# Per-head keys, values and w_in loaded as they are and converted on the engines

## The chip, the cores and the metric

The kernel runs on one core of a Trainium2 chip. Its work is spread over five engines that run at the same time and wait for each other through semaphores: TensorE (PE in the profile, its weight loads PEld), VectorE (DVE), ScalarE (ACT), GpSimd (POOL) and SyncE (SP). DMAs are issued from the instruction queues of SyncE, ScalarE or GpSimd, and their bytes are moved by 16 DMA engines that all issuers share. The metric is the device time of one execution in microseconds; less is better.

## What is computed

A retention layer (attention with a decay instead of a softmax) over 8 batches of 8 heads, 576 positions and 64 features, then a feed-forward layer with a hard-swish between two matrices, over all 4608 tokens:

```python
    batch, n_heads, seq, head_dim = (8, 8, 576, 64)
    n_tokens, d_model, d_ff = (4608, 512, 2048)
...
    scores = scale * np.matmul(q, k.transpose(0, 1, 3, 2))
    gamma = 1.0 - 2.0 ** (-5.0 - np.arange(H, dtype=np.float32))
    rel = pos[:, None] - pos[None, :]
    Dmat = np.where(rel >= 0, gamma[:, None, None] ** rel[None, :, :], 0.0)
    ret = scores * Dmat[None, :, :, :]
    return np.matmul(ret, v).astype(np.float32)
...
    h = x @ w_in
    relu6 = np.clip(h + 3.0, 0.0, 6.0)
    g = h * relu6 / 6.0
    return (g @ w_out).astype(np.float32)
```

All inputs and the output are float32; the matrix products on the chip run on float16 operands, so every operand is converted somewhere on its way.

## The kernel before

The 576 positions of a batch are 64 + 512. The first 64 positions of all eight batches together are one block of 512 tokens, block 0 (the "heads" of the sequences, in names hk, hq, hv). The other 512 positions of each batch are blocks 1 to 8, each cut into four chunks of 128 positions, loaded as fk, fq and fv by `load` (lines 166 to 180). For every block the kernel forms the retention output transposed (`xT`), multiplies it by w_in in 16 units ("up", products `ph`, 8 matmuls a unit), applies the hard-swish on ScalarE and VectorE (lines 514 and 516) and multiplies by w_out ("down", products `pd` and `pm`). From block 2 on the down product uses a Strassen scheme with sums of w_out (`ws`).

The order of work is written out by hand from line 749: `manual_schedule` keeps the instructions of each engine in the order of the text. So an instruction that waits holds up everything that stands behind it in its engine's queue, DMA issues included.

The part that the change touches is the beginning, up to the fifth unit of the up product of block 0:

- `indices` (line 89) and `distances` (line 107): small constants. The distances lie in `early`, a buffer of the tag "fv", which has four (IOB, line 56).
- Loads of the heads (lines 753 to 769): four pairs of batches, i = 0 to 3, each in two halves e. All queries and the first keys are loaded as float32 by SyncE and ScalarE. The keys of pairs 1 to 3 (`load_half`, line 394) and all values (`load_values`, line 439) are issued by GpSimd straight into float16 tiles, so that the DMA converts them. `behind` means that a DMA is issued only after another one has landed (`after`, line 389).
- `win_piece` (line 675) and `wout_piece` (line 683): w_in in four pieces of 512 columns and w_out in four pieces, all issued by GpSimd and converted by the DMA. Piece n of w_in serves the units 4n to 4n + 3 of the up product of block 0.
- `mask_of_heads` (line 115): ScalarE makes the decay masks of two heads a call from the distances; the four calls stand among other ScalarE work.
- `cast_heads` (line 414) converts a float32 head tile on VectorE: the first keys and all queries. `turn_heads` (line 419) transposes keys and queries on PE and copies them back on ScalarE. `picks` (line 435) fills `pick`, a selection matrix that GpSimd cleared before (line 767). `scores_heads` (line 464) forms scores and multiplies them by the masks on VectorE; `values_heads` (line 449) brings the values to chunk order with `pick`; `inner_heads` (line 477) makes `xT`.
- `decays`, `mask_of_chunk`, `decays_of_chunk` (lines 120 to 138): constants that the later chunks need, made on GpSimd behind the w_out issues (lines 817 to 819).
- `fetch(8, wout[0])` (line 820): SyncE loads chunks 4 to 7 once the first piece of w_out has landed.
- `idle_products` (line 379): products that nobody reads.

The order of PE at the beginning is: idle products, turns of keys and queries of pairs 0 to 3 with the scores of the pairs between, values, inner products, then the first four up units side by side, one quarter of the depth at a time, then one unit after another.

Of the kernel before, what the change touches and what calls it, by code (L numbers as in the profile page):

```python
# [12 lines left out]
FP32 = mybir.dt.float32  # L13
# [3 lines left out]
ALU = mybir.AluOpType  # L17
# [4 lines left out]
def kernel(  # L22
# [97 lines left out]
    def decays():  # L120
        for h in range(H):
            lg = float(np.log(gamma[h]))
            nc.gpsimd.tensor_scalar(arg[:, :, h], fj[:, 0:4], lg, float(np.log(D ** -0.5)), ALU.mult, ALU.add)
            nc.gpsimd.tensor_scalar(arg[:, :, H + h], fj[:, 0:4], -lg, 0.0, ALU.mult, ALU.add)
        nc.scalar.activation(dec, arg, ACTF.Exp)
# [268 lines left out]
    def load_half(i, nm, e, queue, behind=None):  # L394

        if nm not in hd.setdefault(i, {}):
            if queue is nc.gpsimd:
                hd[i][nm] = heads16(i, nm)
            else:
                f = half_tile(io, "fq", i, FP32, "hq", bufs=2) if nm == "q" else io.tile(  # L400
                    [P, H * D], FP32, tag=f"f{nm}", name=f"h{nm}{i}")
                hd[i][nm] = f.rearrange("p (e j d) -> p e j d", e=2, j=NJ)
        d = queue.dma_start(hd[i][nm][:, e].rearrange("p j d -> p (j d)"),  # L403
                            dict(q=q, k=k, v=v)[nm][:, 2 * i + e, 0:TL, :].rearrange("b (r j) d -> r b (j d)", j=NJ))
        if behind is not None:
            after(d, behind)
        return d
# [30 lines left out]

    def load_values(i, behind=None):

        t = heads16(i, "v")
        for e in range(2):
            d = nc.gpsimd.dma_start(t[:, e].rearrange("p j d -> p (j d)"),  # L443
                                    v[:, 2 * i + e, 0:TL, :].rearrange("b (r j) d -> r b (j d)", j=NJ))
            if behind is not None:
                after(d, behind)
        hd.setdefault(i, {})["v"] = t
# [227 lines left out]
    def win_piece(n, parts=1, behind=None):  # L675
        a, b = pieces_in[n]
        for i in range(parts):
            cc = slice(NP // parts * i, NP // parts * (i + 1))
            d = nc.gpsimd.dma_start(win16[n][:, cc], win_v[:, cc, BLK * a:BLK * b])  # L679
            if behind is not None:  # L680
                after(d, behind)

# [66 lines left out]
    with tc.manual_schedule(engines={ENG.PE, ENG.DVE, ENG.Pool, ENG.Activation, ENG.SP}):  # L749
        sp, act, pool = nc.sync, nc.scalar, nc.gpsimd  # L750
        on_act, on_dve = nc.scalar.copy, nc.vector.tensor_copy
# [11 lines left out]
        for i in (1, 2, 3):  # L763
            for e in range(2):
                load_half(i, "k", e, pool, None if i == 1 else keys)
            if i == 1:
                nc.gpsimd.memset(pick, 0.0)
        for i in range(NP):
            load_values(i)
        win_piece(0, 2)  # L770
        for n in (1, 2, 3):
            win_piece(n)
        wout = [wout_piece(pc) for pc in (0, 2, 1, 3)]
        distances()
        idle_products(5)
        mask_of_heads(0)
        cast_heads(0, "k", on_dve)
        picks()
        turn_heads(0, "k", on_act)
        mask_of_heads(1)  # L780
        idle_products(4)
        cast_heads(0, "q", on_dve)
        mask_of_heads(2)
        turn_heads(0, "q", on_act)
        cast_heads(1, "q", on_dve)
        turn_heads(1, "k", on_act)
        turn_heads(1, "q", on_act)
        cast_heads(2, "q", on_dve)
        scores_heads(0)
        mask_of_heads(3)  # L790
        idle_products(1)
        turn_heads(2, "k", on_act)
        turn_heads(2, "q", on_act)
        cast_heads(3, "q", on_dve)
        scores_heads(1)
        idle_products(1)
        turn_heads(3, "k", on_act)
# [9 lines left out]
        inner_heads(2, on_dve)  # L807
        first = [up_steps(0, u) for u in range(4)]
# [8 lines left out]
        decays()  # L817
        mask_of_chunk()
        decays_of_chunk()
# [78 lines left out]
```

## Time and profile before

| what | value |
|---|---|
| median of 3 runs | 299.61 us (298.64 to 300.04) |
| the profiled execution's own time | 301.09 us |
| its span, first to last instruction | 299.4 us |
| granted TensorE clock in every stretch | 1.00 |
| DMA, issued by SyncE (hardware queue q1) | 41.56 MB in 114336 packets |
| DMA, issued by GpSimd (software queue q0) | 5.11 MB in 4720 packets |

The 5.11 MB of the GpSimd queue are counted as they land: 6 key halves and 8 value halves of 64 KB, w_in and w_out of 2 MB each, all in float16; read were twice as many bytes.

How the lines are read: a row of the order of time has start and length in us, engine, line, operation, output<-input, shapes, number of instructions, and in brackets how long the engine stood idle before it and what released it. A stretch (A:B) has busy time and number of instructions of PE, PEld, DVE, ACT and POOL in turn, then the granted clock, the mean busy share of the DMA engines (packets overlap, so it can pass 1) and GB/s moved. A line of waits has engine and line, what it waited for, us in total, how often, and the longest.

The DMA queue at the beginning, 0 to 45 us (packets, MB, share of 16 engines' time), and the issues of that time (count, KB each, median us from issue to landing):

```profile
q0 software_dynamic: 4720, 5.11, 70.5%
q1 hardware_dynamic: 7708, 2.99, 26.2%
...
wout<-in_moe_w_out_dram POOLq DMA_DIRECT2D x4, 512.0 KB, 18.9
win<-in_moe_w_in_dram POOLq DMA_DIRECT2D x3, 512.0 KB, 12.5
...
hv<-in_v_dram POOLq DMA_DIRECT2D x8, 64.0 KB, 3.8
win<-in_moe_w_in_dram POOLq DMA_DIRECT2D x2, 256.0 KB, 7.4
hk<-in_k_dram POOLq DMA_DIRECT2D x6, 64.0 KB, 4.5
```

### The profile page before, as it was taken

To read this page: it belongs to the slowest core of one execution; us is meant where nothing else is said; L and a number is where in the kernel's file an instruction comes from. 1 tells how busy PE (TensorE), PEld (TensorE's weight loads), DVE (VectorE), ACT (ScalarE), POOL (GpSimd) and SP (SyncE) were. 2 spreads that over 40 slices of the span, in tenths; PEclk is the share of its full clock that TensorE was granted. 3 is DMA by queue.
4 is the path that set the end of the run, shared out by engine and by line. 5 is a ranking of instruction groups with operands and counts; after the bars stand their busy time and mean duration, and the time that the engine had idled before them with its cause. 6 is when DMAs were issued, how large, how long until landed. Compare 5 with 4: busy or idle time off the path is not lost.

```text
span 299.4 us, 12624 instructions
## 1 busy us (share of the span) xinstructions
PE 287.2 (96%) x5574; PEld 219.8 (73%) x5574; DVE 216.0 (72%) x380; ACT 190.5 (64%) x343; POOL 133.9 (45%) x169
## 2 busy tenths in 40 slices
PE   4998999999999999999989999999999999999995
PEld 2675655877556667898768878988787787778894
DVE  8648768859835678788957796678759776647654
ACT  3738855778866687585767577667766574565420
POOL 8961046656841912529621962296237003100510
PEclk9999999999999999999999999999999999999999
DMA  7999989996999999999999899989908100200114
GB/s 164 148 182 214 231 204 228 242 243 120 186 209 168 246 197 221 172 202 205 239 219 212 147 201 215 151 162 259 141 11 145 73 2 29 102 15 2 72 72 140
DMA packets 119542, 47.86 MB, mean 160 GB/s; under 512 B 92352, under 2 KB 114880, under 8 KB 119488
## 3 DMA queue, kind: packets, MB, share of 16 engines
q1 hardware_dynamic: 114336, 41.56, 71.3%
q0 software_dynamic: 4720, 5.11, 10.6%
q8 instruction: 43, 0.70, 1.0%
q10 hardware_dynamic: 432, 0.39, 0.5%
q14 instruction: 11, 0.09, 0.1%
HBM read 36.70 MB, written 9.44 MB: 154 GB/s over the span
## 4 chain that ended last, share of the span: by engine, by line
PE 77%; DMA 10%; POOL 6%; ACT 3%; DVE 2%; issue 1%; SPq 0%; POOLq 0%; ACTq 0%
PE ph L153 36%; PE pm L153 29%; DMA wout<-in_moe_w_out_dram 5%; PE pd L153 4%; PE po L232 3%; DMA fq<-in_q_dram 3%; PE pa L232 2%; DMA fv<-in_v_dram 2%; POOL hv L443 1%; POOL hk L403 1%; POOL win L679 1%; PE pu L232 1%; POOL q L192 1%; ACT z L327 1%; ACT kT L211 1%
## 5 line engine op out<-in xcount | busy, mean ns | idle before, releaser
L153 PE MATMUL ph<-xT,win 128*64 128x512 f16 (+1 forms) x1248 | 144.5, 364 | 1.5 <-DMA win<-in_moe_w_in_dram 1.5
L516 DVE SCALAR_TENSOR_TENSOR g<-u,ph 128x512 f16<-128x512 f32 x132 | 89.6, 684 | 50.4 <-ACT u L514 49.9
L514 ACT ACTIVATE u<-ph,half 128x512 f32<-128x512 f32 x132 | 90.3, 691 | 42.6 <-PE ph L153 40.1
L153 PEld LDWEIGHTS <-win 128*64 128x64 f16 x1248 | 83.1, 136 | 28.4 <-DMA win<-in_moe_w_in_dram 2.1
L153 PEld LDWEIGHTS <-g 128*64 128x64 f16 x928 | 50.6, 110 | 15.5 <-issue 0.4
L153 PEld LDWEIGHTS <-s 128*64 128x64 f16 x896 | 51.0, 110 | 8.2 <-issue 1.1
L321 POOL TENSOR_TENSOR z<-z,gpow 128x256 f32<-128x256 f32 x24 | 16.2, 673 | 67.5 <-DVE z L320 44.8
L153 PE MATMUL pm<-ws,s 128*64 128x256 f16 x672 | 46.1, 273 | 0.2 <-issue 0.2
L192 POOL TENSOR_TENSOR q<-fq,dec 128x512 f16<-128x512 f32 x30 | 35.6, 1204 | 17.2 <-DMA fq<-in_q_dram 17.2
L195 POOL TENSOR_TENSOR v<-fv,dec 128x512 f16<-128x512 f32 x32 | 36.2, 1134 | 2.6 <-PE ph L153 2.6
L612 POOL TENSOR_TENSOR u<-u,p 128x512 f32<-128x512 f32 x7 | 8.9, 1271 | 62.0 <-ACT u L652 55.8
L373 ACT CAST xT<-po 128x256 f16<-128x256 f32 (+1 forms) x44 | 22.6, 585 | 21.4 <-PE po L232 21.4
L153 PE MATMUL pd<-wout,g 128*64 128x512 f16 x256 | 34.2, 382 | 0.1
L153 PE MATMUL pm<-wout,g 128*64 128x256 f16 x448 | 30.8, 273 | 0.0
L267 DVE TENSOR_TENSOR a<-pa,mask 128x256 f16<-128x256 f32 (+1 forms) x44 | 21.9, 539 | 10.3 <-PE pa L232 6.9
L548 DVE TENSOR_TENSOR s<-g 128x1024 f16<-128x1024 f16 x28 | 19.4, 694 | 0.2
L327 ACT CAST z<-z 128x512 f16<-128x512 f32 x24 | 14.9, 620 | 7.0 <-DVE z L317 6.6
L188 ACT CAST k<-fk 128x512 f16<-128x512 f32 x29 | 18.0, 621 | 1.0 <-DMA fk<-in_k_dram 1.0
L153 PE MATMUL pm<-ws,g 128*64 128x256 f16 x224 | 16.9, 274 | 0.0
L153 PE MATMUL pm<-wout,s 128*64 128x256 f16 x224 | 16.7, 273 | 0.2
L232 PE MATMUL po<-qT,z 64*64 64x64 f16 x512 | 12.6, 198 | 1.3 <-ACT z L327 0.7
L232 PEld LDWEIGHTS <-z 64*64 64x64 f16 x512 | 8.0, 106 | 7.5 <-ACT z L327 2.5
(111 smaller groups left out, 292.6 us busy)
## 6 DMA issues: line engine op xcount, KB each, us to landing
fk<-in_k_dram SPq DMA_DIRECT2D x32, 256.0 KB, 4.7
fq<-in_q_dram SPq DMA_DIRECT2D x16, 512.0 KB, 6.0
fv<-in_v_dram SPq DMA_DIRECT2D x32, 256.0 KB, 5.7
out_dram<-o SPq DMA_DIRECT2D x14, 512.0 KB, 3.6
wout<-in_moe_w_out_dram POOLq DMA_DIRECT2D x4, 512.0 KB, 18.9
out_dram<-o SPq DMA_DIRECT2D x7, 256.0 KB, 5.7
win<-in_moe_w_in_dram POOLq DMA_DIRECT2D x3, 512.0 KB, 12.5
hq<-in_q_dram SPq DMA_DIRECT2D x6, 128.0 KB, 4.7
```

The lines of the kernel that those rows point to most:

```text
L153: nc.tensor.matmul(out[r], lhs[:, r], rhs, skip_group_check=True, **flags)
L188: (nc.gpsimd.tensor_copy if c in K_POOL else nc.scalar.copy)(by_head(k16), in_rows(st[c]["fk"]))
L192: (nc.vector if e and c in Q_DVE else nc.gpsimd).tensor_tensor(by_head(q16[:, e]), in_rows(st[c]["fq"][:, :, e, :]), in_rows(dd[:, 2 + e, ...
L195: nc.gpsimd.tensor_tensor(v16, st[c]["fv"], dd[:, 1, H:2 * H, :], ALU.mult)
L232: return lambda: nc.tensor.matmul(*args, skip_group_check=True, **flags)
L267: nc.vector.tensor_tensor(a16[:, a, 0:n].rearrange("p x i q -> p (x i) q"), pa[a].rearrange("p x i q -> p (x i) q"), m, ALU.mult)
L321: nc.gpsimd.tensor_tensor(new, new, decay, ALU.mult)
L327: nc.scalar.copy(z16, zs[c])
L373: nc.scalar.copy(xt[:, s], po[s].rearrange("p x n (e r) -> p x n e r", e=2))
L514: nc.scalar.activation(uu[:, 0:n], ph[:, 0:n], ACTF.Relu, bias=half, scale=1.0 / 6.0)
L516: nc.vector.scalar_tensor_tensor(out=g[:, hf, ths, jr, :], in0=by_half(uu), scalar=1.0, in1=by_half(ph), op0=ALU.min, op1=ALU.mult)
L548: nc.vector.tensor_tensor(*pend.popleft())
```

## The change

No size, tile or product changes. What moves:

- Keys of pairs 1 to 3 and all values are still issued by GpSimd, but into float32 tiles of the tags "fk" and "fv". VectorE casts the keys, GpSimd the values. The fourth value tile takes the buffer in which the distances lie.
- w_in is issued by SyncE, as float32, in eight DMAs once the values of pair 0 have landed, into buffers that are used later for `g` (pieces 0 and 1) and for output tiles (pieces 2 and 3). GpSimd casts it in 16 instructions of 128x512. w_out stays as it is, but its issues now stand among these casts.
- `pick` is cleared on VectorE, ahead of the second pair's casts; GpSimd makes the chunk mask and its decays in that place instead.
- `decays` (16 small operations) runs on VectorE, behind the first key's cast. All masks of the heads are made at once, ahead of the other ScalarE work.

```diff
     def decays():
         for h in range(H):
             lg = float(np.log(gamma[h]))
-            nc.gpsimd.tensor_scalar(arg[:, :, h], fj[:, 0:4], lg, float(np.log(D ** -0.5)), ALU.mult, ALU.add)
-            nc.gpsimd.tensor_scalar(arg[:, :, H + h], fj[:, 0:4], -lg, 0.0, ALU.mult, ALU.add)
+            nc.vector.tensor_scalar(arg[:, :, h], fj[:, 0:4], lg, float(np.log(D ** -0.5)), ALU.mult, ALU.add)
+            nc.vector.tensor_scalar(arg[:, :, H + h], fj[:, 0:4], -lg, 0.0, ALU.mult, ALU.add)
...
     def load_half(i, nm, e, queue, behind=None):
         if nm not in hd.setdefault(i, {}):
-            if queue is nc.gpsimd:
-                hd[i][nm] = heads16(i, nm)
-            else:
-                f = half_tile(io, "fq", i, FP32, "hq", bufs=2) if nm == "q" else io.tile(
-                    [P, H * D], FP32, tag=f"f{nm}", name=f"h{nm}{i}")
-                hd[i][nm] = f.rearrange("p (e j d) -> p e j d", e=2, j=NJ)
+            f = half_tile(io, "fq", i, FP32, "hq", bufs=2) if nm == "q" else io.tile(
+                [P, H * D], FP32, tag=f"f{nm}", name=f"h{nm}{i}")
+            hd[i][nm] = f.rearrange("p (e j d) -> p e j d", e=2, j=NJ)
...
-    def win_piece(n, parts=1, behind=None):
+    staged = {}
+
+    def win_piece(n, behind=None):
         a, b = pieces_in[n]
-        for i in range(parts):
-            cc = slice(NP // parts * i, NP // parts * (i + 1))
-            d = nc.gpsimd.dma_start(win16[n][:, cc], win_v[:, cc, BLK * a:BLK * b])
+        if n < 2:
+            t = gp.tile([P, NP, BLK], FP32, tag="g", bufs=4, name=f"wf{n}")
+            halves = [t[:, 0:2], t[:, 2:4]]
+        else:
+            halves = [work.tile([P, 2, BLK], FP32, tag=f"o{x}", bufs=2, name=f"wf{n}_{x}") for x in range(2)]
+        for x, t in enumerate(halves):
+            d = nc.sync.dma_start(t, win_v[:, 2 * x:2 * x + 2, BLK * a:BLK * b])
             if behind is not None:
                 after(d, behind)
+        staged[n] = halves
+
+    def win_cast(n, x):
+        for y in range(2):
+            nc.gpsimd.tensor_copy(win16[n][:, 2 * x + y], staged[n][x][:, y])
...
             if i == 1:
-                nc.gpsimd.memset(pick, 0.0)
+                mask_of_chunk()
+                decays_of_chunk()
         for i in range(NP):
-            load_values(i)
-        win_piece(0, 2)
-        for n in (1, 2, 3):
-            win_piece(n)
-        wout = [wout_piece(pc) for pc in (0, 2, 1, 3)]
+            for e in range(2):
+                landed = load_half(i, "v", e, pool)
+            if i == 0:
+                values = landed
+        for n in range(4):
+            win_piece(n, values if n == 0 else None)
         distances()
         idle_products(5)
-        mask_of_heads(0)
+        for i in range(NP):
+            mask_of_heads(i)
         cast_heads(0, "k", on_dve)
-        picks()
         turn_heads(0, "k", on_act)
-        mask_of_heads(1)
+        decays()
         idle_products(4)
         cast_heads(0, "q", on_dve)
-        mask_of_heads(2)
+        nc.vector.memset(pick, 0.0)
         turn_heads(0, "q", on_act)
+        cast_heads(1, "k", on_dve)
         cast_heads(1, "q", on_dve)
+        picks()
         turn_heads(1, "k", on_act)
         turn_heads(1, "q", on_act)
+        cast_heads(2, "k", on_dve)
         cast_heads(2, "q", on_dve)
         scores_heads(0)
-        mask_of_heads(3)
         idle_products(1)
         turn_heads(2, "k", on_act)
         turn_heads(2, "q", on_act)
+        cast_heads(3, "k", on_dve)
         cast_heads(3, "q", on_dve)
         scores_heads(1)
         idle_products(1)
+        for i in range(NP):
+            cast_heads(i, "v", on_pool)
         turn_heads(3, "k", on_act)
...
         inner_heads(2, on_dve)
+        for n in range(2):
+            win_cast(n, 0)
+            win_cast(n, 1)
+        win_cast(2, 0)
+        wout = [wout_piece(pc) for pc in (0, 2)]
+        for n, x in ((2, 1), (3, 0), (3, 1)):
+            win_cast(n, x)
+        wout += [wout_piece(pc) for pc in (1, 3)]
         first = [up_steps(0, u) for u in range(4)]
...
-        decays()
-        mask_of_chunk()
-        decays_of_chunk()
         fetch(8, wout[0])
```

More of the change, by code (lines that the diff above doesn't have):

```diff
@@ L437, in picks @@
             nc.vector.tensor_copy(pick[:, j].rearrange("p c (x j) -> p (c x) j", j=NJ)[:, :, j], by_chunk)
[L439 to L447, printed above, removed]
     def values_heads(i, copy):
@@ L750 @@
         sp, act, pool = nc.sync, nc.scalar, nc.gpsimd
-        on_act, on_dve = nc.scalar.copy, nc.vector.tensor_copy
+        on_act, on_dve, on_pool = nc.scalar.copy, nc.vector.tensor_copy, nc.gpsimd.tensor_copy
         indices()
```

## The prediction

> **What bounds the kernel now.** I read the engine shares first, then PE's busy time by stretches, then PE's waits of the first 60 us, then the order of time from 2 to 24 us. The page's engine line and four of the stretches:
>
> ```profile
> PE 287.2 (96%) x5574; PEld 219.8 (73%) x5574; DVE 216.0 (72%) x380; ACT 190.5 (64%) x343; POOL 133.9 (45%) x169
> ...
> 15.00:20.00 5.00, 4.51 (x130) 3.97 (x126) 3.18 (x5) 1.76 (x4) 2.72 (x7) 1.00 1.14 169
> 20.00:25.00 5.00, 4.02 (x44) 2.53 (x42) 2.19 (x4) 3.35 (x7) 3.56 (x26) 1.00 1.25 208
> 25.00:30.00 5.00, 5.00 (x50) 3.23 (x48) 3.90 (x7) 3.95 (x7) 0.00 (x0) 1.00 1.11 218
> ...
> 60.00:270.00 210.00, 207.41 (x4186) 161.14 (x4187) 155.17 (x264) 143.79 (x255) 94.80 (x93) 1.00 0.87 160
> ```
>
> The second number of a stretch is PE's busy time. From 25 us on PE hardly pauses (207.4 of 210 us later), and its instruction order is fixed. So a start of the up-products that is x earlier or later shifts the end by x; only what happens before about 24 us counts. There, PE's own waits:
>
> ```profile
> PE ph L153 <- DMA win<-in_moe_w_in_dram: 1.5, 2, 1.0
> PE hptq L423 <- ACT hqT L428: 0.2, 1, 0.2
> ```
>
> PE twice waits for w_in: 0.49 us ahead of the first up-product and 0.98 us ahead of the fifth unit. In order of time, the rows that set the front:
>
> ```profile
> 2.26 2.69 DVE L110 TENSOR_SCALAR early<-query,fj 128x128 f32<-128x128 f32 x1
> 3.02 1.84 POOL L767 MEMSET ws<- 128x2048 f16 x1
> 5.65 0.43 DVE L416 CAST hk<-hk 128x512 f16<-128x512 f32 x1
> 6.00 0.82 DVE L437 COPY ws<-by_chunk 128x128 f16<-128x128 f16 x4
> 10.69 0.64 PE L153 MATMUL idle<-ident 128*64 128x512 f16 x2
> 10.87 1.29 DVE L474 TENSOR_TENSOR ha<-hpa,ws 128x512 f16<-128x512 f32 x2 [1.56 <-ACT hqT L428]
> 12.03 0.41 PE L153 MATMUL idle<-ident 128*64 128x512 f16 x2
> 12.07 0.50 DVE L416 CAST hq<-hq 128x512 f16<-128x512 f32 x1
> 12.72 0.41 PE L423 MATMUL hptq<-by_chunk,hq 128*64 128x128 f16 x8
> 13.39 1.08 PE L153 MATMUL hpv<-hv,ws 128*64 128x128 f16 x32
> 18.77 1.95 PE L153 MATMUL ph<-xT,win 128*64 128x512 f16 x16 [0.49 <-DMA win<-in_moe_w_in_dram]
> 23.68 10.58 PE L153 MATMUL ph<-xT,win 128*64 128x512 f16 x96 [0.98 <-DMA win<-in_moe_w_in_dram]
> ```
>
> The last cast of a query (12.07 to 12.57) releases PE's last turn (12.72), and from there PE runs without a break until 18.28. VectorE has idle holes before 10.87, so until then it is not the limit.
>
> **Step 1, the distances (gain 0.5 to 1.8 us on VectorE, I take 1.0).** GpSimd's clearing of `pick` leaves; the chunk mask and decays (22.78 to 24.14 before, 1.4 us) take its place. VectorE's line 110 began at 2.26 and ended at 4.95, just behind that clearing (4.86); the remaining distances end at 5.73, 0.78 later. If line 110 gets in right at 3.1, they end at 3.9; if only behind the new GpSimd work at 4.4, at 5.2. I take 4.7. The first keys had landed at 3.84 by the trace's landing records.
>
> **Step 2, the decays on VectorE (0 on the path).** Sixteen tensor_scalar of 128x4: small VectorE operations start about 0.065 us apart (L95 to L100, 1.09 to 1.40), 1.0 us; at most their length of 0.15 each, 2.4. They stand behind the first key's cast: 4.7 + 0.45 + 1.0 = 6.2. The next cast needs the first queries, whose second half landed at 6.81, so this hides under that landing, and the cast ends at 7.3 as now (6.90 + 0.43). At the dear end 0.7 shows.
>
> **Step 3, clearing and key casts on VectorE (loss).** Behind it in VectorE's queue: the clearing of `pick`, the second pair's key and query casts, picks, the third pair's two casts, the first scores' two masks, the fourth pair's two casts. No row clears 2,048 elements on VectorE. Low: two of the 1,024-element f16 sums of line 548, 0.68 each, 1.4. High: four masks of 512 at 0.62, 2.5. I take GpSimd's 1.84, the nearest row. Casts are 0.45 each from start to start, picks 0.82. So 7.3 + 1.8 + 0.9 + 0.8 + 0.9 = 11.7; masks 1.25 to 13.0; the last two casts to 13.9, where before the last ended at 12.57: **+1.35 us** (0.9 to 2.0). [...]
>
> **Step 4, values cast on GpSimd (0, with a collision of 0.3).** In before, GpSimd's issues of the eight value loads ended at 11.6 and the halves landed from 10.98 to 15.81. Line 188 casts such a tile on GpSimd in 0.61. The four then end at about 12.2, 13.2, 14.0 and 16.4, while PE, 1.35 later, wants them at 14.7, 16.1, 17.2 and 18.3: hidden. Without that cover the last would cost up to 0.6. But a VectorE f16 sum takes 0.68 alone and up to 1.52 beside GpSimd work (line 548), so one GpSimd cast may hold a VectorE cast for 0.6: 0 to 1.2, I take half of one, **+0.3**. The fourth value load must also wait for the buffer that holds the distances, so for the eight masks on ScalarE: 4.7 + 8 x 0.32 = 7.3, ahead of its issue near 10. Masks taken together also put ScalarE's first copy at 7.3 rather than 6.81; PE's next copy is due only at about 9.9, so 0.
>
> **Step 5, w_in (gain).** SyncE issues eight loads once the first value pair has landed (11.31); before, GpSimd issued them from 11.55 behind all values. Nothing else stands in SyncE's queue until the chunk loads. Landings before: 18.73 and 19.98 for the two halves of piece 0, then 23.64, 26.2 and 28.7: 2.5 us a piece once running, with a thin stretch from 13.3 to 17.5. Packets of 1,024 bytes from 2,048 took 98 ns; stores of 2,048 unconverted took 84. So the new loads should run no slower: 2.5 us a piece from 14.3 gives 16.8, 19.3, 21.8, 24.3. Four GpSimd casts of 0.6 a piece, behind the values' last at 16.4, end at 18.8, 21.7, then, with the issues of two w_out pieces (0.6 each) in the midst of piece 2, at 25.4 and 27.8. PE reaches the first up-product at 18.28 + 1.35 + 0.3 = 19.9 and the fifth unit 3.9 later (18.77 to 22.70 before), at 23.8; pieces 2 and 3 are due at 27.3 and 30.7. All are ready, so both waits go: **-1.47**. The bad end is rival A.
>
> **Step 6, the clock (loss 0 to 1.7, I take 0.4).** The granted clock reads 1.00 throughout, yet the two idle products of 512 took 0.64 at 10.69 and 0.41 at 12.03, and single-operand spacing fell from 0.106 to 0.055 us at 11.2. PE had then worked almost without gaps since 6.13, for 5.1 us. Now PE has nothing from about 8 to 9.9, while VectorE clears and casts. Counted anew from 9.9 it speeds up at 15.0; PE is paced by VectorE until about 14.3, so 0.7 at half speed costs 0.4.
>
> **Step 7, w_out and chunk loads (0, down to -0.5).** The first w_out piece landed at 31.17 and released the chunk loads; now it is issued behind ten w_in casts, at about 23, and should land by 28. GpSimd's 17.2 us wait for the queries of chunk 4 shrinks, but PE waited only 0.2 there, and was idle 0.5 from 40 to 60 us in all.
>
> **Sum.** +1.35 + 0.3 - 1.47 + 0.4 = +0.6 us. The profiled execution took 301.09 us with a span of 299.4; its span becomes 300.0. The median of the runs shown is 299.61, so I state **300.2 us**, own range 299.0 to 301.2.
>
> **Rivals.** **A, w_in no sooner than before, conversion behind it (0.20).** It decides if piece 1 lands after about 21.4, so that its four casts (2.4 us) end after PE's arrival at 23.8. If it lands at 23.64 as before, casts end at 26.05 and unit 5 ends about 26.3 against 24.54: +1.75, **301.4**. For it: values and w_in now share the DMA engines (busy share 0.97 to 1.25 between 10 and 25 us). Against: the thin stretch, which other issuing may avoid. **B, the clock stays low (0.20).** If the slow spacing lasts until 17.7 or so, the dense stretch from 14.3 loses 3.4/2 = 1.7 rather than 0.4: +1.9, **301.5**. For it: the new hole in PE's work. [...] **C, VectorE does not become the limit (0.15).** If clearing costs little (0.5 us) and the distances end at 3.9, the last query cast ends near 12.6 and only the -1.47 is left: **298.1**. For it: VectorE's holes of 0.35, 0.68 and 1.56 us before 10.87. Against: line 767's 1.84 and three key casts added to the same stretch.
>
> **How the numbers follow.** Forecast 0.45, A 0.20, B 0.20, C 0.15. A measurement of this kernel can tell about 0.5% (1.5 us) from no change, so the bounds are 298.1 and 301.1. Of the forecast 0.33 lies within, 0.08 above, 0.04 below; of A 0.05 within, 0.15 above; of B 0.03 and 0.17; of C half below. That makes faster 0.11, same 0.49, slower 0.40. The range 298.3 to 302.3 reaches to the middle of C, and over A and B to their own spread.
>
> **What would show it.** Right: a clearing of about 1.8 us on VectorE, the last query cast ending near 13.9, the first up-product near 20 with no wait for w_in or its casts, unit 5 near 24, one unit each 0.86 after. Wrong: PE waiting on GpSimd's line of casts (A), slow spacing beyond 15 us (B), the last query cast at 12.6 (C); or a stop after 30 us that is not there now, which no step has.

## The result and the profile after

| | before | after |
|---|---|---|
| median | 299.34 us of 4 runs (298.64 to 300.04) | 314.10 us of 4 runs (313.02 to 315.50) |
| profiled execution, and its span | 301.09, 299.4 us | 314.55, 312.8 us |

The ratio is 1.0496 (95% interval 1.0444 to 1.0547): the change costs about 5%, 14.8 us by the medians and 13.46 us between the two profiled executions. The prediction (300.2 us, range 298.3 to 302.3) was wrong.

The engine line of the page after, and the stretches that the prediction showed of before (columns as there):

```profile
PE 290.0 (93%) x5574; PEld 223.3 (71%) x5574; DVE 220.7 (71%) x400; ACT 190.1 (61%) x343; POOL 137.9 (44%) x167
```

```profile
15.00:20.00 5.00, 4.43 (x50) 2.54 (x48) 4.84 (x23) 4.22 (x12) 3.51 (x5) 1.00 1.00 360
20.00:25.00 5.00, 3.23 (x36) 1.61 (x36) 5.00 (x9) 1.28 (x3) 5.00 (x9) 1.00 1.02 374
25.00:30.00 5.00, 4.89 (x98) 3.92 (x96) 3.76 (x7) 1.75 (x3) 4.95 (x9) 1.00 0.98 179
60.00:270.00 210.00, 205.89 (x4312) 159.23 (x4298) 157.08 (x268) 144.59 (x259) 102.04 (x101) 1.00 0.88 162
```

PE works as densely behind 60 us as before (205.9 of 210 us). The loss is at the front: from 15 to 25 us PE starts 86 products where before it started 174, while VectorE and from 20 us GpSimd are busy without a pause. The DMA view of 0 to 45 us shows that the loads changed as meant; its 2.99 MB of the hardware queue have become 6.89:

```profile
q1 hardware_dynamic: 9176, 6.89, 51.9%
q0 software_dynamic: 1248, 3.93, 39.7%
...
wf<-in_moe_w_in_dram SPq DMA_DIRECT2D x8, 512.0 KB, 8.4
```

The waits of the first 35 us (engine and line, what it waited for, us in total, how often, the longest):

```profile
PE hptk L420 <- DVE hk L413: 12.7, 3, 10.7
ACT ws L118 <- DVE early L113: 10.9, 1, 10.9
DVE early L110 <- POOL hv L413: 10.4, 1, 10.4
```

PE's wait for w_in is gone, as intended. Instead the first turn of the keys waits 10.7 us for the first key cast, and ScalarE's masks 10.9, both because VectorE stands still for 10.4 us at line 110, the first operation of the distances. It is released by a GpSimd cast of values. VectorE in order of time (start, length, ..., in brackets the idle time before and what ended it):

```profile
12.70 0.29 DVE L110 TENSOR_SCALAR early<-query,fj 128x128 f32<-128x128 f32 x1 [10.37 <-POOL hv L413]
...
13.90 0.58 DVE L113 SCALAR_TENSOR_TENSOR early<-query,fj,early 128x128 f32<-128x128 f32 x1
14.40 0.41 DVE L413 CAST hk<-hk 128x512 f16<-128x512 f32 x1
14.74 0.58 DVE L123 TENSOR_SCALAR arg<-fj 128x4 f32<-128x4 f32 x1
...
16.86 0.91 DVE L783 MEMSET ws<- 128x1024 uint32 x1 [0.16 <-issue]
...
17.97 0.82 DVE L413 CAST hq<-hq 128x512 f16<-128x512 f32 x1
18.72 2.62 DVE L434 COPY ws<-by_chunk 128x128 f16<-128x128 f16 x4
21.17 0.92 DVE L413 CAST hk<-hk 128x512 f16<-128x512 f32 x1
...
22.75 1.27 DVE L461 TENSOR_TENSOR ha<-hpa,ws 128x512 f16<-128x512 f32 x2
...
24.61 0.83 DVE L413 CAST hq<-hq 128x512 f16<-128x512 f32 x1
```

GpSimd beside it:

```profile
12.05 0.61 POOL L413 CAST hv<-hv 128x512 f16<-128x512 f32 x1 [0.53 <-DMA hv<-in_v_dram]
...
16.78 7.63 POOL L679 CAST win<-wf 128x512 f16<-128x512 f32 x10 [1.49 <-DMA wf<-in_moe_w_in_dram]
...
25.55 3.38 POOL L679 CAST win<-wf 128x512 f16<-128x512 f32 x6
```

Two things are to be seen. Line 110 starts when GpSimd's cast of the first values (12.05 to 12.66) is done: a wait that the kernel before does not have. And since VectorE's casts come so late, five of the eight now run beside GpSimd's casts of w_in and its issues of w_out: such a cast takes 0.75 to 0.92 us instead of 0.43, the four copies into `pick` 2.62 instead of 0.82. From the first key cast to the end of the last query cast it takes 11.04 us (14.40 to 25.44), before 6.92 (5.65 to 12.57).

**Where the time goes.** PE's order of products is the same in all these kernels (but for a few neighbours behind product 400 that change places in e6, e7 and e9), so the start of the same product can be compared. The table gives the start before, and for every kernel the difference to it, in us; the products are counted from 0 and named by the group in which they lie (the row of 10 is the first product of the first turn; 340 lies in the eighth unit). The rows of the experiments are used below.

```
product        10      90     130     256     340     600    5573
          1st turn last key 1st value 4th value unit 8 chunks    last
before       6.13   12.39   13.98   17.72   26.97   44.98  295.69
after       +8.73  +12.57  +13.69  +14.30  +12.36  +11.93  +13.46
e1          -1.67   +0.93   +1.60   +1.61   -0.34   +2.09   +3.14
e2         +14.72  +14.58  +14.53  +15.88  +13.93  +13.53  +14.77
e4          -0.01   -0.26   -0.20   +0.84   -0.42   +9.28   +7.24
e5          -1.67   +1.29   +5.72   +7.93   +5.99   +5.57   +6.60
e6          -1.71   +1.03   +1.31   +2.82   +0.88   +0.47   +2.41
e7          -1.73   +0.57   +0.65   +2.57   +0.63   +0.23   +2.41
e8          -0.02   +0.39   +0.31   +2.19   +0.25   +1.25   +0.37
e9          +9.27   +9.48   +9.50  +11.11   +9.19   +8.78   +9.84
e10         -0.03   -0.57   -0.53   +0.64   +0.59   +1.11   +0.09
e11         -0.03   -0.57   -0.53   -0.53   +1.30   +1.81   +1.83
e12         -1.67   +1.33   +1.40   +1.43   -0.51   -0.94   -2.31
e13         -0.03   -0.25   -0.20   -0.20   +1.29   +1.83   +0.01
```

For the changed kernel: +8.73 up to the first turn (the distances), +3.84 more up to the last key turn (VectorE), +1.73 up to the fourth values (of it 0.84 because the first 32 value products took 1.92 us instead of 1.08: the same products at a slower pace, see the last section), then -1.94 as the waits for w_in are gone, -0.43 up to the chunks, and +1.53 behind them, of which the last section accounts for 1.41. The sum is +13.46. (By the medians all differences are larger, since the profiled execution of before, 301.09 us, lies above the median of its runs.)

### The profile page after: what moved, and what is told of

It reads as the page before. It is cut to its first block, busy times and chain, and to the rows that moved or that the text cites. A ratio compares the mean times of both kernels' runs of the same rounds, so it can differ in the third digit from the quotient of the medians.

```text
span 312.8 us, 12661 instructions
## 1 busy us (share of the span) xinstructions
PE 290.0 (93%) x5574; PEld 223.3 (71%) x5574; DVE 220.7 (71%) x400; ACT 190.1 (61%) x343; POOL 137.9 (44%) x167
## 4 chain that ended last, share of the span: by engine, by line
PE 80%; DVE 5%; DMA 4%; POOL 4%; ACT 3%; issue 2%; SPq 0%; POOLq 0%; DVEq 0%; ACTq 0%
PE ph L153 38%; PE pm L153 28%; PE pd L153 5%; PE po L232 3%; DMA fv<-in_v_dram 3%; PE pa L232 2%; DMA hv<-in_v_dram 2%; PE hpv L153 2%; PE pu L232 1%; POOL hk L400 1%; DVE hq L413 1%; POOL v L195 1%; ACT kT L211 1%; DVE ws L434 1%; DVE g L503 1%
## 5 line engine op out<-in xcount | busy, mean ns | idle before, releaser
L153 PEld LDWEIGHTS <-win 128*64 128x64 f16 x1248 | 84.8, 136 | 25.0 <-issue 0.3
L153 PEld LDWEIGHTS <-g 128*64 128x64 f16 x928 | 51.6, 110 | 16.1 <-issue 1.9
L195 POOL TENSOR_TENSOR v<-fv,dec 128x512 f16<-128x512 f32 x32 | 35.5, 1112 | 4.3 <-DMA fv<-in_v_dram 4.3
L373 ACT CAST xT<-po 128x256 f16<-128x256 f32 (+1 forms) x44 | 22.6, 586 | 21.4 <-PE po L232 21.4
L420 PE MATMUL hptk<-by_chunk,hk 128*64 128x128 f16 x32 | 2.5, 314 | 12.8 <-DVE hk L413 12.7
```

The source lines that it names most:

```text
L153: nc.tensor.matmul(out[r], lhs[:, r], rhs, skip_group_check=True, **flags)
L195: nc.gpsimd.tensor_tensor(v16, st[c]["fv"], dd[:, 1, H:2 * H, :], ALU.mult)
L373: nc.scalar.copy(xt[:, s], po[s].rearrange("p x n (e r) -> p x n e r", e=2))
```

## The experiments

None changes a product or leaves any of the computation out. Each was compared with the kernel before on the same chip. The theory after the result: a buffer of the tag goes to the tile whose first writing instruction comes first in the text. The tile of the distances is declared at line 80, ahead of all loads, but the first instruction that writes it, line 110, stands behind the loads of the four value tiles. With four buffers of that tag it gets the one that the first values have taken; so line 110 waits until these have landed and been cast, and all of VectorE, ScalarE's masks and PE's turns stand behind it. The section on the change says that the fourth value tile takes the buffer of the distances; by this theory it is the other way round, the distances take over a buffer of the values.

### e1_own_buffer: a buffer of their own for the distances

```diff
-    early = io.tile([P, H, D], FP32, tag="fv", name="early").rearrange("p h d -> p (h d)")
+    early = const.tile([P, 2 * P], FP32, name="early")
```

> The changed kernel, with the distances in a buffer of their own. Theory A (the distances took over the buffer of the first values and so waited for these to land and be cast, and all else of the front is late because of it): the distances end near 5 us instead of 14.5, the last query cast near 14 instead of 25.4, the first up-product near 20 instead of 32.4, and the time falls to about 300 (299 to 302), 1.0 us or less from the kernel before. [...] Rival C (the added casts and clearings on VectorE and their collisions with GpSimd's casts cost several us in any case): the distances end near 5, but the time stays at 303 or more.

Measured: 304.04 us (6 runs), ratio 1.0158 (1.0115 to 1.0202). The first turn is 10.4 us earlier than in the changed kernel, and 10 of the 14.8 us are gone. So the buffer is the main cause, but not the whole one: 4.3 us stay. The time is the one that rival C gave (303 or more), but not for its reason, VectorE's added work: PE's eighth unit is ahead of before. By the table, w_in brings what it was to bring (1.95 us from the fourth values to unit 8, which is 0.34 us ahead of before), and between there and the chunks 2.4 us are lost. PE's and GpSimd's waits say on what:

```profile
PE ptq L153 <- POOL q L192: 1.7, 1, 1.7
...
POOL q L192 <- DMA fq<-in_q_dram: 13.4, 1, 13.4
```

GpSimd scales the queries of a chunk, which have landed late, and PE waits for it.

### e2_win_by_dma and e5_own_win_by_dma: w_in converted by the DMA again

e2 is the changed kernel with this edit; e5 has the buffer of e1 as well.

```diff
-        for n in range(4):
-            win_piece(n, values if n == 0 else None)
+        win_piece(0, 2)
+        for n in (1, 2, 3):
+            win_piece(n)
+        wout = [wout_piece(pc) for pc in (0, 2, 1, 3)]
...
-        (GpSimd's casts of w_in)
```

> The changed kernel, buffer still shared, but w_in converted by GpSimd's DMAs as in the kernel before, so that no w_in casts run on GpSimd. It asks what stretched VectorE from its first key cast (14.4 us) to its last query cast (25.4), 11.0 us against 6.9 before. [...] Rival C (the added VectorE work alone): the stretch stays at 11 and the time at 314.

> Both edits: the changed kernel with the distances in a buffer of their own and w_in converted by GpSimd's DMAs. What remains of the change is keys and values cast on the engines, and the clearing and decays on VectorE. Theory A: the front is 1 to 2 us later than before by VectorE's added work, PE's w_in waits shrink by as much, so 299 to 301. Rival C: 303 or more, as in the first of these runs by its own reading.

Measured: e2 316.63 us (4 runs), ratio 1.0570 (1.0513 to 1.0626); e5 307.24 us (6 runs), 1.0240 (1.0191 to 1.0289). VectorE in e2:

```profile
18.29 0.60 DVE L110 TENSOR_SCALAR early<-query,fj 128x128 f32<-128x128 f32 x1 [15.96 <-POOL hv L413]
...
23.86 0.74 DVE L434 COPY ws<-by_chunk 128x128 f16<-128x128 f16 x4
```

In e2 GpSimd must issue w_in and w_out before it casts values, so the first values are cast at 18 us, and the distances follow them there: the later the cast, the later the distances. That shows the wait a second time, by its size. With no w_in casts beside it, VectorE's stretch from the first key cast to the last query cast takes 6.73 us (20.38 to 27.11) instead of 11.04, and the copies into `pick` 0.74. So the slow VectorE work of the changed kernel is due to GpSimd's casts beside it; e6 shows the same with the casts of the values. In e5 the late value casts hit PE directly: it waits 3.9 us for them at the first value products (+1.29 at the last key, +5.72 at the first values). e2 was expected near 311 and e5 at 299 to 301; both took longer, because neither expectation saw that GpSimd's issues would hold up the casts of the values.

### e4_win_by_sync: of the change, w_in alone

The kernel before with the change's `win_piece`, its `win_cast` and their places in the queues; keys, values, decays and masks as before.

> The kernel before, with nothing of the change but w_in: issued by SyncE unconverted behind the first values, cast on GpSimd, w_out issued among these casts; keys and values as before. Theory A (the prediction's step on w_in was right, only hidden): both of PE's waits for w_in (1.5 us) go and the time falls by about 1.5 us, to 0.995 of the kernel before. Rival D (w_in lands no sooner or its casts come late): PE waits for the casts, time same or up to 1.7 us more.

Measured: 308.12 us (6 runs), ratio 1.0290 (1.0250 to 1.0329). PE's fifth unit starts 1.1 us earlier; 0.68 goes back to a wait within units 5 to 8 for GpSimd's casts, and then PE loses 9.7 us. The waits from 26 to 46 us:

```profile
DVE g L517 <- ACT u L515: 12.3, 6, 9.9
ACT dec L125 <- POOL arg L124: 9.8, 1, 9.8
...
PE ph L153 <- DVE g L517: 6.7, 1, 6.7
```

The decays stand on GpSimd behind the casts of w_in; ScalarE's exponential waits for them, ScalarE's `u` waits behind that, and so VectorE and PE. This is what the change's move of the decays to VectorE prevents. Neither expectation had this wait.

### e6_text_order: distances and masks asked for ahead of the values

```diff
+        distances()
+        idle_products(5)
+        for i in range(NP):
+            mask_of_heads(i)
         for i in range(NP):
             for e in range(2):
                 landed = load_half(i, "v", e, pool)
...
-        distances()
-        idle_products(5)
-        for i in range(NP):
-            mask_of_heads(i)
```

> The changed kernel, with the distances, their idle products and the four mask calls moved in the text ahead of the value loads; the distances still take a buffer of the tag fv, no tile, size or product changes, and on each engine the order is the same but for the value loads, which now ask for a buffer later than the distances do. Theory (who takes the buffer first decides who waits): the distances get an unused buffer, end near 3.5 us instead of 14.5, PE's first turn starts near 4.5; in their place the fourth pair's value loads wait for the eight masks, which end near 7, ahead of their issue: time 302 to 305, as with a buffer of its own (304.0). Rival (sharing costs wherever the distances stand): a GpSimd issue now waits, w_in and w_out issues behind it slip, and the time is 308 or more. Rival (the late distances have another cause): 314.

Measured: 303.07 us (4 runs), ratio 1.0101 (1.0061 to 1.0142). The tag still has four buffers for five tiles. VectorE, ScalarE and GpSimd in order of time:

```profile
2.25 0.28 DVE L110 TENSOR_SCALAR early<-query,fj 128x128 f32<-128x128 f32 x1
...
12.46 0.77 DVE L413 CAST hk<-hk 128x512 f16<-128x512 f32 x1
13.15 0.83 DVE L413 CAST hq<-hq 128x512 f16<-128x512 f32 x1
```

```profile
3.55 2.43 ACT L118 ACTIVATE ws<-early,scale 128x128 f16<-128x128 f32 x8
```

```profile
9.81 2.48 POOL L400 DMA_DIRECT2D hv<-in_v_dram  x3 [0.20 <-issue]
12.34 2.11 POOL L413 CAST hv<-hv 128x512 f16<-128x512 f32 x3
```

The distances begin at 2.25 and the masks end at 5.98, long before GpSimd issues the fourth values from 11.2 on: now it is the fourth values that would have to wait for the buffer, and they don't. Line 80, where the tile is declared, stays where it was; moving four lines of text that use it, with every instruction kept, is worth 11 us, and the time is within the range expected. The first turn is where it is with a buffer of its own (-1.71, -1.67). The two casts at 12.46 and 13.15 run beside GpSimd's casts of values and take 0.8 instead of 0.43.

### e7_own_wout_early: e1, and all of w_out behind the second piece of w_in

```diff
-        for n in range(2):
-            win_cast(n, 0)
-            win_cast(n, 1)
-        win_cast(2, 0)
-        wout = [wout_piece(pc) for pc in (0, 2)]
-        for n, x in ((2, 1), (3, 0), (3, 1)):
-            win_cast(n, x)
-        wout += [wout_piece(pc) for pc in (1, 3)]
+        for n in range(4):
+            if n == 2:
+                wout = [wout_piece(pc) for pc in (0, 2, 1, 3)]
+            win_cast(n, 0)
+            win_cast(n, 1)
```

> The changed kernel with a buffer of their own for the distances (304.0), and all four w_out pieces issued by GpSimd behind the casts of w_in's second piece instead of two behind the fifth cast and two behind the last. Theory (the late w_out pieces push the chunk loads back, and with them the 2.4 us that PE lost from 38 to 45 us): the last w_out pieces land sooner, ahead of the chunk loads, GpSimd waits less for the queries of chunk 4, PE's gap at 38 to 45 us goes: 301.5 to 302.5. Rival (w_out now shares the DMA engines with w_in's last pieces and chunk loads are late for their volume): w_in's third piece is late for PE by 1 to 2 us, time 304 to 306.

Measured: 303.64 us (4 runs, 300.40 to 304.67), ratio 1.0103 (1.0038 to 1.0167), so the time of the forecast was missed. The step itself came as expected: from unit 8 to the chunks PE gains 0.40 us where e1 loses 2.43, and GpSimd's wait for the queries falls from 13.4 to 10.9. What e1 lost there was due to late w_out pieces and chunk loads. But this profile has a new stop of 1.95 us behind product 222, for which the profile names no releaser ("issue"); it is taken up below.

### e9_values_alone: of the change, the values alone

```diff
-            if queue is nc.gpsimd:
+            if queue is nc.gpsimd and nm == "k":
...
-            load_values(i)
+            for e in range(2):
+                load_half(i, "v", e, pool)
+        for i in range(NP):
+            cast_heads(i, "v", pool.tensor_copy)
```

> The kernel before with one change: the values are loaded as float32 into tiles of the tag fv and cast on GpSimd right behind their issues, ahead of the issues of w_in; keys, w_in, masks and decays as before. Theory (the distances get the buffer of the first values): line 110 waits for the landing and the cast of the first values, distances end 8 to 10 us later than before (5.7), PE's first turn 8 to 9 us later, but no w_in casts run beside VectorE's, so from the first key cast to the last query cast it takes about 7 us, not 11; w_in is there in time and its 1.5 us of waits are gone: 305 to 308. Rival (values and buffer harmless): 299 to 301.

Measured: 311.30 us (4 runs), ratio 1.0376 (1.0333 to 1.0419). VectorE and GpSimd:

```profile
12.54 0.71 DVE L110 TENSOR_SCALAR early<-query,fj 128x128 f32<-128x128 f32 x1 [10.20 <-POOL hv L416]
```

```profile
11.87 1.94 POOL L416 CAST hv<-hv 128x512 f16<-128x512 f32 x3
```

The values alone bring the wait (10.2 us; first turn +9.27), and with no w_in casts VectorE's stretch takes 7.25 us (14.52 to 21.77). Both are as expected; the waits for w_in are gone too (-1.92 from the fourth values to unit 8). The time lies 3.3 us above the range expected; 1.61 of it is the stop at product 222, which occurs here too, and the rest is not taken apart.

### e8_win_by_sync_decays: e4 with the decays ahead of the casts

```diff
+        decays()
+        mask_of_chunk()
+        decays_of_chunk()
         distances()
...
+        nc.scalar.activation(dec, arg, ACTF.Exp)
         fetch(8, wout[0])
```

(The exponential is taken out of `decays` and stays in its old place on ScalarE.)

> The kernel before with w_in alone loaded by SyncE and cast on GpSimd (that was 308.1), and the decays' small operations, the chunk mask and its decays moved on GpSimd ahead of those casts, the exponential on ScalarE where it was. Theory (the 9.9 us lost at 35 us was ScalarE waiting for the decays behind the casts, and w_in's gain of 1.5 us is real): the stall is gone, PE waits for no w_in, the fifth up unit starts 0.4 to 1.4 us earlier than before, and what is left of a loss is the chunk loads: 298.5 to 301. Rival (GpSimd's casts cost more than that place): a new wait for GpSimd's work behind them, 303 or more.

Measured: 300.74 us (11 runs; a twelfth took 304.39), ratio 1.0044 (1.0015 to 1.0074). The stop of e4 is gone, and PE waits for no w_in. From the fourth values to unit 8 PE gains 1.94 us. It has lost them before, at one place in PE's order of time:

```profile
18.94 0.41 PE L483 MATMUL hpo<-ha,ws 128*64 128x128 f16 x8 [1.66 <-DVE ws L455]
```

The releaser shown (VectorE's copy, done at 17.1) had long finished: this is again the stop at product 222. So the fifth unit is +0.30, not ahead of before as the theory said. The time is within its range.

### e10, e11 and e13: e8 with w_out early, and w_in held back

e10 is e8 with the edit of e7. e11 and e13 are e10 with w_in's first loads behind the third and the fourth pair of values:

```diff
-            if i == 0:
+            if i == 2:        # e13: 3
                 values = d
```

> The kernel before with w_in by SyncE and the decays ahead of its casts (that was 300.8, with a stop of 1.7 us on TensorE at its 223rd product), and the four w_out pieces issued behind the casts of w_in's second piece. Theory (a. the stop is TensorE's next block of instructions, whose 16 KB transfer began only 0.5 us before TensorE came to its end; b. the late w_out pieces and chunk loads cost 0.4 to 0.8 us at 40 us): b goes, the stop stays or not by the start of that transfer: 299 to 300.5; with no stop 298.5. Rival (w_out now delays w_in's third piece): a wait for w_in or its casts of 1 to 2 us, 301 to 302.

> The run before this one, with one change: w_in's first loads wait for the third pair of values instead of the first. Theory (TensorE's block of instructions comes late because w_in's transfers fill the DMA engines from 14 us on): between 13 and 17 us the engines carry less, the block's transfer begins 1 to 2 us sooner (15 to 16 us), the stop at the 223rd product shrinks to under 1 us; w_in comes 1 to 2 us later, and PE waits for it or its casts by 0 to 1.5 us: 298.5 to 300.5. Rival (the start of that transfer has nothing to do with w_in): it begins at 16.8 to 17.4 as in three runs before, the stop stays at 1.5 us or more, and the time is 300 to 302.

> As the run two before this one, with w_in's first loads waiting for the last pair of values. Theory (w_in's transfers delay TensorE's block of instructions): the thin stretch of the kernel before (13.3 to 17.5 us) is back, the block's transfer begins at 14 to 15.5 us as it did there (14.3), and there is no stop at the 223rd product; w_in now comes 3 to 4 us later than by the first pair of values, and its casts end behind PE's arrival: waits of 2 to 4 us, 301 to 303. Rival (nothing to do with w_in): transfer at 16.8 to 17.4 and a stop of 1.5 us besides those waits, 303 to 305.

Measured: e10 301.18 us (12 runs), ratio 1.0053 (1.0025 to 1.0080); e11 301.44 (12 runs), 1.0051 (1.0029 to 1.0073); e13 302.00 (4 runs), 1.0089 (1.0054 to 1.0123). PE and GpSimd in e10:

```profile
24.36 8.88 PE L152 MATMUL ph<-xT,win 128*64 128x512 f16 x68 [1.10 <-POOL win L692]
```

```profile
23.68 1.17 POOL L692 CAST win<-wf 128x512 f16<-128x512 f32 x2 [1.70 <-DMA wf<-in_moe_w_in_dram]
```

In e10 the stop at product 222 is down to 0.34 us, and the fifth unit starts 1.1 us ahead of before. There PE meets w_in: the second half of its second piece has landed only at 23.63, and with its casts PE is 0.59 behind before at unit 8; another 0.98 go to the third piece, cast behind the four w_out issues (the rival's wait). Between unit 8 and the chunks e10 loses 0.52 us where e8 loses 1.00, so the early w_out helped there. Nothing is won in all, and the time is the rival's.

PE's wait for w_in's casts in e11:

```profile
PE ph L152 <- POOL win L692: 2.8, 3, 1.4
```

In e11 and e13 the stop at product 222 is gone, as the theory wanted, and the waits for w_in's casts take its place; e11 lies 0.9 us above its range, e13 within. Whether holding w_in back removed the stop is not settled, as the last section shows.

### e12_keys_alone: of the change, the keys alone

The kernel before with the keys of pairs 1 to 3 as float32, their casts and the clearing of `pick` on VectorE, and the chunk's mask and decays on GpSimd in the place of the clearing.

> The kernel before with the keys alone: those of pairs 1 to 3 loaded as float32 and cast on VectorE, the selection matrix cleared on VectorE and copied behind the second pair's casts, the chunk mask and its decays on GpSimd where the clearing was; values, w_in, decays and masks as before. It is the prediction's first and third steps by themselves. By the prediction: distances end at 3.9 to 5.2, the last query cast at 13.9 instead of 12.57, PE's first up product later by up to 1.35 less the 0.49 that it waits for w_in anyway, then less the 0.98 ahead of the fifth unit: 299.5 to 300.2. By the run in which the distances had a buffer of their own (clearing 0.9 us, last query cast at 13.3): +0.7 at that cast, all of it inside the waits for w_in: 299.3 to 300.0. Rival (key casts on VectorE are dear by themselves): last query cast at 14.5 or later and 301 or more.

Measured: 300.70 us (12 runs), ratio 1.0033 (1.0013 to 1.0054). VectorE:

```profile
8.34 0.91 DVE L783 MEMSET ws<- 128x1024 uint32 x1 [0.16 <-issue]
...
12.83 0.46 DVE L416 CAST hq<-hq 128x512 f16<-128x512 f32 x1
```

PE's last turn of the keys, here and in the kernel before:

```profile
13.51 0.64 PE L423 MATMUL hptk<-by_chunk,hk 128*64 128x128 f16 x8
```

```profile
12.27 0.39 PE L423 MATMUL hptk<-by_chunk,hk 128*64 128x128 f16 x8
```

The last query cast ends at 13.29, +0.72 to before, by the second of the two expectations; PE is 1.40 later at the first values. The rest is PE's own: from 9.58 to 13.93 it works without a pause at the slow pace, which ends at 14.0 here and at 11.2 before. All of it is made up where PE waited for w_in before: unit 8 is 0.51 ahead. The median is 0.8 us above before, 0.5 above the first of the two ranges expected and 0.7 above the second, and below the rival's 301; the profiled execution happens to be the shortest of the twelve, so its trace does not show where the median's 0.8 us lie.

No version beat the kernel before; e8, e10, e11 and e12 lie 0.3 to 0.5% above it.

## Why the prediction was wrong, step by step

- **What bounds the kernel**: right. PE's order is fixed and an early shift reaches far (+11.93 at product 600, +11.94 at product 2100); behind that the stops of the last section, which the prediction did not have, move the end by up to 2 us (e4: +9.28 at the chunks, +7.24 at the last product).
- **Step 1, the distances (gain 1.0, ending at 4.7): the step that failed.** They end at 14.48, behind a wait of 10.4 us at line 110. Without the shared buffer (e1, e6, e12) they end at about 3.43, earlier than forecast, since line 110 takes 0.28 us instead of the 2.69 that it took beside GpSimd's clearing. The prediction saw that five tiles share four buffers, but in step 4 it put the wait on the wrong side: it had the fourth values wait for the distances. The buffer goes to the tile that the text writes first, and the text writes the distances behind all values, though they come first in time. e1 and e6 show it from two sides, e2 and e9 by the distances following the first value cast.
- **Step 2, the decays (0)**: right in e6, where they lie at 4.29 to 5.63 ahead of the first queries (7.71). In the changed kernel the cover is gone: they stand between key and query cast (14.74 to 16.37).
- **Step 3, clearing and key casts (+1.35)**: right in kind. The clearing took 0.91, below its low end: its row shows 1,024 elements of uint32, where GpSimd's row of before (1.84) has 2,048 of f16. The last query cast ends at 13.29 in e12 and 13.98 in e6 (forecast 13.9).
- **Step 4, values on GpSimd (+0.3)**: a term mis-sized. Beside the casts of values two VectorE casts cost 0.75 more (e6). In the changed kernel the delay puts five of VectorE's casts beside GpSimd's work on w_in and w_out: its eight casts and the copies into `pick` take 8.0 us there and 4.2 alone (8 x 0.43 and 0.74), so 3.8 us.
- **Step 5, w_in (-1.47)**: right in the changed kernel, e1, e6 and e8, where PE waits for none of it and gains 1.94 to 1.95. But PE comes late to it there (1.6 us or more); where it does not (e4, e10), part of the gain goes back. The halves landed at 18.0, 21.4, 24.3 and 26.9 (second halves, trace's landing records), 3.0 us a piece rather than 2.5, and 1.2 to 2.6 later than forecast, still in time.
- **Step 6, the clock (+0.4)**: right in kind, its size different in each kernel. That the slow pace is counted anew for 5.1 us behind a hole was the author's estimate from one reading (6.13 to 11.2 in before). On the first 32 value products it cost 0 in e6 and e12 (1.08), 0.36 in e1 (1.44) and 0.84 in the changed kernel (1.92); in e12 it cost about 0.7 ahead of them. In the changed kernel PE stayed slow up to 29.1 us, though the last hole of over 0.15 us in its work (1.54 us) ended at 22.14; why so long, no run shows.
- **Step 7, w_out and chunks (0 to -0.5)**: wrong in sign for e1 (+2.43), -0.43 in the changed kernel, where PE is so late that the loads are in time.
- **Rivals**: none decided the time. A's mechanism is real: in e10 half of the second piece lands at 23.63, after the 21.4 from which A was to decide, and PE waits. In the changed kernel the delay of step 1 hides it. B's slow clock is the 0.84; that it ends at 17.7 no run shows, the first clock record begins at 8.8 in e10, 12.1 in e8 and 29.1 in the changed kernel. C's early last cast did not come (13.26 to 13.98 without the wait, forecast 13.9). All four cases shared step 1, so none of them had a stop ahead of the first turn.

## What to carry to other kernels

When a change puts more tiles under a tag, write down the order in which the text first writes its tiles (not the order in which it declares them), and for each the last reader of the tile that had the buffer before: a tile that is needed first but written last in the text waits for all of that. A moved load or cast is worth what the stretch allows that it lands in: the same w_in casts cost VectorE nothing behind its work and, with w_out's issues, 3.8 us beside it. And an operation that looks dear in a row (2.69 us) can be a short one (0.28) that runs beside another engine's work.

## What the runs showed that was not expected

**TensorE's stops and the instruction queue.** Where PE stops without a releaser ("issue", or a releaser long done), it is at one of the same products in every kernel: 222, 862, 1246, 2398, 2654, 2910, 3550 or 4446, give or take six, all 222 plus a multiple of 128. All 27 idle times of PE over 0.3 us that the 14 profiles put down to "issue" behind its first product lie there. The page after, DMA queues:

```profile
q8 instruction: 43, 0.70, 1.0%
```

This queue moves 43 blocks of 16,384 bytes; PE has 5,574 products and as many weight loads, 259 a block. The stop is taken here as the longest time between the starts of two neighbouring products at a boundary (0.05 where there is none at 222), PE's arrival as the first of these two starts. Setting each block's start (from the trace's packet records) against PE's arrival at its boundary, over the 14 profiles and 588 boundaries: where the transfer began less than 2.0 us ahead of PE's arrival (31 times), PE stopped each time, for 0.42 to 1.95 us, and lead and stop add up to 2.25 to 2.96 us; where it began more than 2.3 us ahead (550), a stop above 0.45 us was seen six times, four of them waits for w_in's casts, the other two at leads of 2.33 and 2.44 us. Product 222 (the expectations of e10, e11 and e13 give these starts by a zero that lies 0.31 us earlier: 14.3, 16.8, 17.4):

```
             block starts  PE arrives  stop
before          14.04        16.72     0.05
e7              17.05        17.42     1.95
e8              16.53        17.05     1.88
e9              25.54        26.30     1.61
e6              17.11        18.08     1.54
e2              30.28        31.30     1.37
e4              15.22        16.52     1.07
e10             14.19        16.19     0.34
e11             13.37        16.08     0.05
e13             13.82        16.41     0.05
```

A row of e6 shows such a stop, eight products of one line cut after the first:

```profile
18.08 0.22 PE L470 MATMUL hpo<-ha,ws 128*64 128x128 f16 x1
19.62 0.38 PE L470 MATMUL hpo<-ha,ws 128*64 128x128 f16 x7 [1.32 <-issue]
```

That the blocks are PE's next instructions is read from this pairing and from the name of the queue; the trace puts no engine beside it. In the profiles these stops make up 3.40 us of the changed kernel (0.72, 1.48 and 1.20) and 1.99 of before (0.44, 1.21 and 0.34); the difference, 1.41, is most of the +1.53 behind the chunks. What sets a block's start stays open: it was early when w_in was held back (e11, e13), but also in e10, which differs from e8 only behind that time.

**VectorE beside GpSimd.** Casts of VectorE took 0.75 to 0.92 us instead of 0.43, and the four copies into `pick` 2.62 us instead of 0.74, while GpSimd cast float32 tiles. GpSimd's casts took longer too: 0.76 us each up to 24.41 and 0.56 from 25.55 on (3.38 for six). Not all of VectorE's work was slowed: two products of scores and masks took 1.27 us beside these casts (22.75) and 1.29 in before, and the clearing 0.91 there and in e12. Each of the four copies took 0.66 us, near the 0.76 of one GpSimd cast (7.63 / 10); by what GpSimd's casts slow them, and whether VectorE stood still for a whole cast, no row shows.

**The clock's record.** In e1 the granted clock reads 0.50 from 10 to 15 us:

```profile
10.00:15.00 5.00, 5.00 (x74) 3.41 (x71) 4.54 (x10) 3.08 (x6) 4.74 (x8) 0.50 0.90 249
```

In the changed kernel it reads 1.00 in every stretch although the same products took 1.92 us instead of 1.08. That 1.00 is no record: the trace's first clock record begins at 29.1 us there and at 11.2 in before, in both cases where the products become faster (turns of one operand 0.10 to 0.11 us apart ahead of it, 0.05 to 0.06 behind it), and for the time ahead of it the view prints 1.00. Up to the first record the length of a known group of products is the sign to go by. When the fast pace begins also differs between runs: e8 and e10 differ in no instruction ahead of 24 us, but the first record begins at 12.1 us in e8 and at 8.8 in e10, and the last key lies at +0.39 and -0.57. So two profiles can differ there by a microsecond without a cause in the kernel.
